# Low parts of expert weights and one-hots on VectorE, reordering copies on ScalarE, in an attention, mixture-of-experts and GLU kernel

## The chip, the cores and the metric

One Trainium2 chip, one core. The metric is the device time of one execution in microseconds (us). TensorE is PE, VectorE is DVE, ScalarE is ACT, GpSimd is POOL, SyncE is SP.

## What is computed

The reference is a chain of three layers on 2304 tokens of width 512 (4 batches of 576):

```python
scores = scale * np.matmul(q, k.transpose(0, 1, 3, 2))
scores = np.where(masks[None], scores, -1e9)      # 4 heads: window 32; 4 heads: dilated by 4
attn = softmax(scores); x = np.matmul(attn, v)    # then heads side by side: (2304, 512)
noisy_logits = x @ w_gate + np.log1p(np.exp(x @ w_noise)) * noise
top2 = np.argpartition(-noisy_logits, 2, axis=1)[:, :2]     # 2 of 8 experts per token, softmax weights
out[mask] += top2_w[mask, k, None] * (np.maximum(x[mask] @ w1[e], 0.0) @ w2[e])
return silu(x @ w_gate2) * (x @ w_val) @ w_out    # GLU, inner width 1536
```

## The kernel before

**Attention** is cut into 36 units (4 batches of 9); a unit has four heads and 128 queries (two blocks of 64, each against 96 keys). `att_step(i)` (L712 on) interleaves three of them, and every engine runs its instructions in the order written: PE scores S(i+1) (L194, L201); DVE row maximum `nm` (L209) and `nb` (L213); PE AV(i-1) (L238); DVE `den`, `rec`, `xs` of unit i-1 (L267 to L273); PE transposes XT(i-2) of `xs` (L284); ACT copies them to `xTb` (L292); PE transposes T(i) of `p` (L227), ACT `pT` (L229); ACT exponentials `p` of unit i+1 (L220). 

**Routing** of each batch (gate logits, two best experts, slots) is a generator, `routing(gi)`; calls of `go(n)` and `pump` between the attention's DVE instructions let it issue n more of its own, so its small DVE operations stand among those of the units. Its last steps build one-hots: per pair (column i of the group, choice k) an `ob` (L463) and an `oa` (L466), which PE multiplies (`s_inv`, L478) to invert the slots. A group has n = 4 or 5 columns, so 2n pairs; POOL builds the last two pairs of each group and DVE the others. `s_rows` (L423 to L455) follows.

**Mixture of experts** runs over steps of one segment (a run of up to 640 slots of an expert) and one eighth f of the inner width. A step's weights `raw` (128x1024) come by DMA (3 buffers) and are split into a high part `whi` (ACT, L173) and a low part `wlo = raw - whi` (L175), 4 buffers each. `moe_step(i)` issues `load_raw(i+5)`, `moe_h(i)` (PE, L657), `hhi` (ACT, L669) and `hlo` (DVE, L670), the token chunks of the next segment (`trans_x`), `split(i+2)` and `moe_y(i-1)` (PE, L696). The low part is DVE's, but POOL's for the four splits that are issued within attention, and for i = 3, 5, 7, 9.

**`trans_x`** reorders a gathered chunk `xg` to `xk` (POOL, L643), transposes it on PE (L608) and makes `xth` (ACT, L616) and `xtl` (DVE, L618). It does so for seven chunks: two of segment 0 (in units 32 and 33, `FIRST_X`), two of segment 1 and three of segment 2. Later segments are turned by DVE and have no such copy.

**Where the work is put** in attention: `LOADS` lists the units in which the first five `raw` are loaded, `SPLITS` those in which the first four are split; the split stands behind the unit's `att_step`, so `whi` is behind the exponentials of the next unit on ACT, and `wlo` ahead of the next unit's `nm` on its engine. The GLU follows after the 88 steps of the experts and is not touched.

Of the kernel before, what the change touches and what calls it, by code (L numbers as in the profile page):

```python
# [8 lines left out]
F32 = mybir.dt.float32  # L9
# [4 lines left out]
AF = mybir.ActivationFunctionType  # L14
OP = mybir.AluOpType
# [25 lines left out]
def attn_moe_glu_kernel(ctx, tc, qT, kT, vB, cst, wgn, noise, wm, wz, out):  # L41
    nc = tc.nc
    V, A, T, G, SP = nc.vector, nc.scalar, nc.tensor, nc.gpsimd, nc.sync
# [96 lines left out]
    iotb = gp.tile([128, 128], BF16, name="iotb")  # L140
    iotc = gp.tile([128, NA * E], BF16, name="iotc")
# [19 lines left out]
    raw, whi, wlo = {}, {}, {}  # L161

    def load_raw(i):
        if i < len(steps):
            s, f = steps[i]
            raw[i] = ring.tile([128, 1024], F32, tag="raw", bufs=3, name="raw")
            SP.dma_start(raw[i], wm[segs[s][0], f])

    def split(i, eng=V):
        if i < len(steps):  # L170
            whi[i] = ring.tile([128, 1024], F32R, tag="whi", bufs=4, name="whi")
            wlo[i] = ring.tile([128, 1024], F32R, tag="wlo", bufs=4, name="wlo")
            A.activation(whi[i], raw[i], AF.Copy)  # L173
            yield
            eng.tensor_tensor(wlo[i], raw[i], whi[i].bitcast(F32), op=OP.subtract)  # L175


    units = []
# [130 lines left out]
    def routing(gi):  # L309
        g0, g1 = groups[gi]  # L310
        n = g1 - g0
        X = {}

        def tl(nm, shape, dt=F32):
            X[nm] = gp.tile(shape, dt, tag="g_" + nm, bufs=1, name="g_" + nm)
            return X[nm]
# [138 lines left out]
            V.tensor_tensor(wm_[:, 0, g0:g1], wm_[:, 0, g0:g1], ov, op=OP.add)  # L455
            yield

        def onehots(eng, pairs):
            if "ob" not in X:
                tl("ob", [128, 2 * n, 128], F16)  # L460
                tl("oa", [128, 2 * n, NA * E], F16)
            for i, k in pairs:
                eng.tensor_scalar(X["ob"][:, 2 * i + k, :], iotb, X["sb"][:, k, i:i + 1], None,  # L463
                                  op0=OP.is_equal)
                yield
                eng.tensor_scalar(X["oa"][:, 2 * i + k, :], iotc, X["ca"][:, k, i:i + 1],  # L466
                                  tokid[:, g0 + i:g0 + i + 1], op0=OP.is_equal, op1=OP.mult)
                yield

        pool = [(i, 1) for i in range(n - 2, n)]  # L470
        mine = [(i, k) for i in range(n) for k in range(2) if (i, k) not in pool]
        order = mine + pool

        def s_inv(pairs):
            iv = X["f"][:, 256:256 + NA * E]
            for pr in pairs:
                j = 2 * pr[0] + pr[1]
                T.matmul(iv, lhsT=X["ob"][:, j, :], rhs=X["oa"][:, j, :], start=pr == order[0],  # L478
                         stop=pr == order[-1], skip_group_check=True)
# [34 lines left out]
        yield NEXT  # L514
        s_rank()
        yield from s_slot()
        for _ in onehots(G, pool):
            pass
        h = len(mine) // 2
        yield from onehots(V, mine[:h])  # L520
        yield NEXT
        A.activation(X["ex"], X["ex"], AF.Exp)
        for _ in range(LAG):
            yield
        s_inv(mine[:h])
        yield from onehots(V, mine[h:])
        yield NEXT
        for _ in range(LAG):
            yield
        s_inv(mine[h:] + pool)  # L530
        yield from s_acc()
        if gi == 3:
            yield NEXT
# [35 lines left out]
    def pump_on(n=99):  # L569
        if route:  # L570
            route[0][1] = True
            pump(n)
# [14 lines left out]
    def by_dve(s):  # L587
        return DVE_SEGS[0] <= s < DVE_SEGS[1]
# [4 lines left out]
    def by_chunk(g):  # L593
        return g.rearrange("p (g k q) -> p k g q", g=4, k=4)

    def spread(g):
        return g.rearrange("p k (g q) -> p k g q", g=4)

    def turned(g, quarter, o=None):

        if quarter:
            flat = g.rearrange("p t c -> p (t c)")
            V.transpose(flat, flat)  # L603
            return g.rearrange("p t (k q) -> p k t q", k=4)
        if o is None:
            o = bank("e").rearrange("p (k q) -> p k q", k=4)
        for c in range(4):
            T.transpose(o[:, c, :] if len(o.shape) == 3 else o[:, c // 2, c % 2, :], g[:, c, :], ident)  # L608
        return o
# [24 lines left out]
    def trans_x(s, a, o=None):  # L634
        e, lo, hi = segs[s]
        if s not in xth:
            xth[s] = mp.tile([128, 4, CAP], F32R, tag="xth", bufs=2, name="xth")
            xtl[s] = mp.tile([128, 4, CAP], F32R, tag="xtl", bufs=2, name="xtl")
        c0 = slice(a * 128 - lo, a * 128 - lo + 128)
        g = xgt.pop((s, a))  # L640
        if not by_dve(s):
            rows, g = g, mp.tile([128, 4, 128], F32, tag="y", bufs=5, name="xk")
            G.tensor_copy(spread(g), by_chunk(rows))  # L643
        src = turned(g, by_dve(s), o)
        yield
        yield from parts(src, xth[s][:, :, c0], xtl[s][:, :, c0], by_dve(s))
# [216 lines left out]
    def moe_step(i):  # L863
        s, f = steps[i]
        last = s == len(segs) - 1
        load_raw(i + 5)
        if i == CVS[0]:
            cv = pools["cv"] = st_cv.enter_context(tc.tile_pool(name="cv", bufs=1, reuse_waits="tile"))
            least.append(cv.tile([128, 1], F32, name="least"))
            V.memset(least[0], 1.125 * 2.0 ** 25)  # L870
        if last and f == 0:
            pools["x2"] = st_x2.enter_context(tc.tile_pool(name="x2", bufs=1, side="right", reuse_waits="tile"))
            load_w2(0, pools["x2"])
            load_w2(1, pools["x2"])
        fg = f - 3 if s == 1 else f
        ft = f - 5 if s == 1 else f - 2
        if not last:
            b0, b1 = segs[s + 1][1] // 128, segs[s + 1][2] // 128
            if 0 <= fg < b1 - b0:
                gather_x(s + 1, b0 + fg)  # L880
        if last and 1 <= f < 4:
            gather_y(f - 1)
        if last and 5 <= f:
            join_y(f - 5)
        if i > 0:
            moe_h(i)
        if i > 2:
            pump_on(3)
        moe_relu(i)
        go(5)  # L890
        tx = trans_x(s + 1, b0 + ft) if not last and 0 <= ft < b1 - b0 else iter(())
        sp = split(i + 2, G if i < 11 and i % 2 else V) if i >= 2 else iter(())
        if by_dve(s + 1):
            next(sp, None)
            next(tx, None)
            next(tx, None)
        else:
            list(tx)
            if last and 6 <= f:
                trans_y(f - 6)  # L900
            next(sp, None)
        if segs[s][2] - segs[s][1] <= LOW:
            list(sp)
            list(tx)
        if i > 0:
            moe_y(i - 1)
            if f == 0:
                moe_out(s - 1)
        if i == 3:
            pump_on(1)  # L910
        go(5)
        if i == 31:
            assert not route
            st_gate.close()
        if i in CVS:
            list(cv_tick(CVS.index(i)))
            if i == CVS[-1]:
                st_cv.close()
        list(tx)
        list(sp)  # L920
# [1 line left out]

    SETS = {(1, 0): (0, 1), (1, 1): (3, 2), (2, 0): (8, 2), (2, 1): (13, 2), (3, 0): (18, 2), (3, 1): (24, 2)}
    coming = {}
    LOADS = (15, 17, 19, 23, 25)
    SPLITS = (20, 22, 24, 26)
    for i in range(-1, NU + 2):
        u = i + 1
        b, r = divmod(u, 9)
        for bt, (i0, di) in SETS.items():  # L930
            if i == i0:
                coming[bt] = load_qkv(*bt)
            if bt in coming and (i - i0) % di == 0:
                next(coming[bt], None)
        if i == 2:
            SP.dma_start(ccon[:, 128:C_MASK], cst[:, 128:C_MASK])
            SP.dma_start(wg, wgn)
            SP.dma_start(nz, noise)
        if 11 <= i < 38:
            if (i - 11) % 9 == 0:  # L940
                route.append([routing((i - 11) // 9), False])
            turn = 99 if len(route) > 1 else 1
        else:
            turn = 0
        if i == NU - 1:
            moe_h(0)
        att_step(i, turn)
        if i >= NU - 1:
            moe_step(i - NU + 1)
        if i < 1:  # L950
            busy(WARM[i + 2])
        if i == 6:
            late_consts()
        if i in LOADS:
            load_raw(LOADS.index(i))
        if i in SPLITS:
            list(split(SPLITS.index(i), G))
        if i == 30:
            gather_x(0, 0)
            gather_x(0, 1)  # L960
# [16 lines left out]
    with tc.If(rv > CAP // 128):  # L977
        with tc.tile_pool(name="ov", bufs=1) as ov:
# [5 lines left out]
            with tc.For_i(0, E, 1) as e:  # L984
                with tc.For_i(CAP // 128, rv, 1) as a:
                    ic = ov.tile([128, 1], I32, tag="ic", name="ic")
                    V.tensor_copy(ic, idx[:, bass.ds(a * E + e, 1)])
                    g = ov.tile([128, DM], F32, tag="xg", name="xg")
# [24 lines left out]
            with tc.For_i(LOW // 128, NT, 1) as t:  # L1013
                for k in range(2):
# [4 lines left out]
                    g = ov.tile([128, DM], F32, tag="xg", name="xg")  # L1019
# [169 lines left out]
```

## Time and profile before

| | |
|---|---|
| three runs | 1068.84, 1066.98, 1057.93 us (median 1066.98) |
| the profiled execution | 1065.96 us |
| its span (first to last instruction) | 1063.9 us, mean granted clock of TensorE 0.984 |
| PE busy | 1024.8 us (96%) |
| DVE busy | 600.0 us (56%) |
| ACT busy | 427.2 us (40%) |
| POOL busy | 331.5 us (31%) |

Times in rows are us from the start of the span. A clock of 1.00 is TensorE's full 2.4 GHz, 0.5 is its lower level, 1.2 GHz. In a row of the timeline the brackets hold the engine's idle time just before the instruction and what ended it; instructions of one kind that follow each other are joined (x4).

### The profile page before, as it was taken

What the parts mean: (1) busy time and instruction counts of PE and PEld (TensorE: products, weight loads), DVE (VectorE), ACT (ScalarE), POOL (GpSimd) and SP (SyncE); (2) the same over time, 40 slices, a digit from 0 to 9 for tenths busy, and PEclk for the clock granted to TensorE, in tenths of its full rate; (3) what the DMA queues carried; (4) which work ended last, traced back from release to release, by engine and by line L of the source; (5) the groups of instructions that cost most, each with busy time, mean ns of one, the idle gap of its engine ahead of it and who ended that gap; (6) DMA issues with size and microseconds to landing.
All of it is one profiled execution on the core that took longest, in us unless ns stands there. A gap on an engine that the chain in (4) does not pass through costs nothing. (4 is left out here: it accounts for less than half of the span.)

```text
span 1063.9 us, 16850 instructions
## 1 busy us (share of the span) xinstructions
PE 1024.8 (96%) x6561; PEld 920.1 (86%) x6562; DVE 600.0 (56%) x1259; ACT 427.2 (40%) x840; POOL 331.5 (31%) x324
## 2 busy tenths in 40 slices
PE   8988988899999999999999999799999999999998
PEld 5776777788999989899989899699999999999997
DVE  3587685468898788897865443134244233343222
ACT  4786543355565555565544322123122122122111
POOL 0023347626343526260001477315126035000000
PEclk8998999999999999999999999899999999999999
DMA  9994355566677777867686586101101101000000
GB/s 252 260 281 148 105 162 179 198 201 187 243 266 254 240 238 242 285 221 238 219 294 223 209 299 228 58 10 40 40 13 43 35 20 40 30 1 1 30 1 30
DMA packets 60980, 161.33 MB, mean 152 GB/s; under 512 B 10048, under 2 KB 17344, under 8 KB 60224
## 3 DMA queue, kind: packets, MB, share of 16 engines
q1 hardware_dynamic: 47904, 120.95, 35.4%
q0 software_dynamic: 12560, 38.82, 11.1%
q8 instruction: 52, 0.85, 0.3%
q10 hardware_dynamic: 432, 0.44, 0.1%
q14 instruction: 32, 0.26, 0.1%
HBM read 121.37 MB, written 38.80 MB: 151 GB/s over the span
## 5 line engine op out<-in xcount | busy, mean ns | idle before, releaser
L591 POOL DMA_INDIRECT xg<-zd,idx x139 | 158.0, 1137 | 168.4 <-DVE xtl L618 127.3
L591 POOL DMA_INDIRECT yg<-zd,row x126 | 122.8, 974 | 200.4 <-DVE yg L844 128.3
L657 PE MATMUL bA<-xth,whi 128*128 128x320 f32 (+2 forms) x452 | 115.9, 314 | 11.9 <-DVE hlo L670 6.1
L657 PE MATMUL bA<-xtl,whi 128*128 128x320 f32 (+2 forms) x452 | 114.9, 312 | 0.2 <-issue 0.2
L657 PE MATMUL bA<-xth,wlo 128*128 128x320 f32 (+2 forms) x452 | 114.6, 311 | 0.0
L1054 DVE TENSOR_TENSOR t<-bB,ex 128x384 f32<-128x384 f32 x36 | 20.1, 558 | 152.6 <-ACT ex L1052 137.8
L669 ACT ACTIVATE hhi<-bA 128x640 fp32r<-128x640 f32 (+2 forms) x73 | 42.4, 581 | 155.7 <-PE bA L657 129.2
L175 DVE TENSOR_TENSOR wlo<-raw,whi 128x1024 fp32r<-128x1024 f32 x80 | 97.2, 1215 | 8.9 <-ACT whi L173 7.7
L657 PEld LDWEIGHTS bA<-xth,whi 128*128 128x128 f32 x452 | 80.6, 190 | 20.8 <-DVE hlo L670 9.2
L173 ACT ACTIVATE whi<-raw 128x1024 fp32r<-128x1024 f32 x88 | 92.7, 1054 | 0.0
L670 DVE SCALAR_TENSOR_TENSOR hlo<-bA,hhi 128x640 fp32r<-128x640 f32 (+2 forms) x73 | 48.9, 669 | 74.8 <-ACT hhi L669 59.1
L657 PEld LDWEIGHTS bA<-xtl,whi 128*128 128x128 f32 x452 | 79.3, 190 | 1.4 <-issue 0.5
L657 PEld LDWEIGHTS bA<-xth,wlo 128*128 128x128 f32 x452 | 79.5, 190 | 0.0
L1052 ACT ACTIVATE ex<-bB 128x384 f32<-128x384 f32 x36 | 17.7, 492 | 151.7 <-PE bB L1046 120.5
L1058 ACT ACTIVATE th<-t 128x384 fp32r<-128x384 f32 x72 | 37.9, 526 | 87.7 <-DVE t L1055 71.8
L1054 DVE TENSOR_TENSOR t<-bA,ex 128x384 f32<-128x384 f32 x36 | 20.1, 558 | 93.3 <-ACT ex L1052 82.3
L1059 DVE TENSOR_TENSOR tl<-t,th 128x384 fp32r<-128x384 f32 x72 | 40.3, 559 | 42.7 <-ACT th L1058 40.9
L1046 PE MATMUL bA<-x2h,wl 128*128 128x384 f32 x288 | 57.7, 340 | 4.6 <-issue 4.6
L1046 PE MATMUL bB<-x2h,wh 128*128 128x384 f32 x288 | 57.3, 341 | 0.0
L1046 PE MATMUL bA<-x2h,wh 128*128 128x384 f32 x288 | 56.5, 338 | 0.3 <-PEq L977 0.3
L1046 PE MATMUL bB<-x2h,wl 128*128 128x384 f32 x288 | 56.4, 337 | 0.0
L1046 PE MATMUL bB<-x2l,wh 128*128 128x384 f32 x288 | 56.3, 337 | 0.0
(233 smaller groups left out, 2353.3 us busy)
## 6 DMA issues: line engine op xcount, KB each, us to landing
raw<-in_wm SPq DMA_DIRECT2D x88, 512.0 KB
r<-in_wz SPq DMA_DIRECT2D x36, 512.0 KB
zd<-y SPq DMA_DIRECT2D x40, 256.0 KB
whd<-cvh SPq DMA_DIRECT2D x36, 256.0 KB
wld<-cvl SPq DMA_DIRECT2D x36, 256.0 KB
wh<-whd POOLq DMA_DIRECT2D x12, 768.0 KB
wl<-wld POOLq DMA_DIRECT2D x12, 768.0 KB
v<-in_vB SPq DMA_DIRECT2D x7, 877.5 KB
```

The costliest lines, as they stand in the source:

```text
L173: A.activation(whi[i], raw[i], AF.Copy)
L175: eng.tensor_tensor(wlo[i], raw[i], whi[i].bitcast(F32), op=OP.subtract)
L591: G.indirect_dma_start(out=g, out_offset=None, in_=src, in_offset=bass.IndirectOffsetOnAxis(ap=ix, axis=0))
L657: T.matmul(hp[:, q, 0:cw], lhsT=wt[:, ws], rhs=xt[:, c, q * cw:q * cw + cw], start=c == 0 and j == 0, stop=c == 3 and j == 2)
L669: A.activation(a3, hp, AF.Relu)
L670: V.scalar_tensor_tensor(l3, hp, 0.0, a3.bitcast(F32), op0=OP.max, op1=OP.subtract)
L1046: T.matmul(p[:, q, 0:LOW], lhsT=w[:, ws], rhs=x[:, c, :], start=c == 0 and j == 0, stop=c == 3 and j == 2, skip_group_check=True)
L1052: A.activation(ex, p[:, 0, 0:LOW], AF.Sigmoid)
L1054: V.tensor_tensor(t, p[:, 0, 0:LOW], ex, op=OP.mult)
L1058: A.activation(a, t, AF.Copy)
L1059: V.tensor_tensor(l, t, a.bitcast(F32), op=OP.subtract)
```

## The change

Every low part is DVE's, every one-hot is DVE's (the pairs are now cut in two equal halves of n), the reordering copy `xk` is ACT's, and the loads and splits within attention lie in other units.

```diff
-    def split(i, eng=V):
+    def split(i):
...
             A.activation(whi[i], raw[i], AF.Copy)
             yield
-            eng.tensor_tensor(wlo[i], raw[i], whi[i].bitcast(F32), op=OP.subtract)
+            V.tensor_tensor(wlo[i], raw[i], whi[i].bitcast(F32), op=OP.subtract)
...
-                eng.tensor_scalar(X["ob"][:, 2 * i + k, :], iotb, X["sb"][:, k, i:i + 1], None,
+                V.tensor_scalar(X["ob"][:, 2 * i + k, :], iotb, X["sb"][:, k, i:i + 1], None,
...
-        pool = [(i, 1) for i in range(n - 2, n)]
-        mine = [(i, k) for i in range(n) for k in range(2) if (i, k) not in pool]
-        order = mine + pool
+        order = [(i, k) for i in range(n) for k in range(2)]
...
-        for _ in onehots(G, pool):
-            pass
-        h = len(mine) // 2
-        yield from onehots(V, mine[:h])
+        yield from onehots(order[:n])
...
-        s_inv(mine[:h])
-        yield from onehots(V, mine[h:])
+        s_inv(order[:n])
+        yield from onehots(order[n:])
...
-        s_inv(mine[h:] + pool)
+        s_inv(order[n:])
...
-            G.tensor_copy(spread(g), by_chunk(rows))
+            A.activation(spread(g), by_chunk(rows), AF.Copy)
...
-        sp = split(i + 2, G if i < 11 and i % 2 else V) if i >= 2 else iter(())
+        sp = split(i + 2) if i >= 2 else iter(())
...
-    LOADS = (15, 17, 19, 23, 25)
-    SPLITS = (20, 22, 24, 26)
+    LOADS = (13, 15, 17, 20, 23)
+    SPLITS = (18, 19, 27, 28)
...
-            list(split(SPLITS.index(i), G))
+            list(split(SPLITS.index(i)))
```

On DVE, around the end of unit 18, the kernel before has the end of group 0's one-hots, the maximum of unit 20 (`nm`), `den` of unit 18 and the copy of the inverted slots:

```order
L463 TENSOR_SCALAR g_ob<-iotb,g_sb 128x128
L466 TENSOR_SCALAR g_oa<-iotc,g_ca,ccon 128x144
L209 TENSOR_REDUCE nm<-bA 128x4
L213 TENSOR_SCALAR nb<-nm 128x4
L267 TENSOR_SCALAR den<-bd 128x4
L484 COPY inva<-bf 128x144
```

The changed kernel has there (its line numbers are 2 to 5 lower in these functions):

```order
L463 TENSOR_SCALAR g_ob<-iotb,g_sb 128x128
L175 TENSOR_TENSOR wlo<-raw,whi 128x1024
L209 TENSOR_REDUCE nm<-bA 128x4
L466 TENSOR_SCALAR g_oa<-iotc,g_ca,ccon 128x144
L213 TENSOR_SCALAR nb<-nm 128x4
L267 TENSOR_SCALAR den<-bd 128x4
L482 COPY inva<-bf 128x144
```

The first `wlo` has come to stand ahead of `nm` and of the group's last `oa`. One unit later the second `wlo` stands in the same way ahead of the next `nm`.

On ACT, in units 31 to 33, the kernel before has the exponentials `p`, the copies `xTb`, the first chunk's `xth` and `pT`:

```order
L220 ACTIVATE p<-bA,nb 128x96 x4
L292 ACTIVATE xTb<-bd 128x2x128
L616 ACTIVATE xth<-bB 128x4x128
L229 ACTIVATE pT<-bc 96x512
L220 ACTIVATE p<-bB,nb 128x96 x4
L292 ACTIVATE xTb<-be 128x2x64 x2
```

The changed kernel has there:

```order
L220 ACTIVATE p<-bA,nb 128x96 x4
L638 ACTIVATE xk<-xg 128x512
L292 ACTIVATE xTb<-bd 128x2x128
L611 ACTIVATE xth<-bB 128x4x128
L229 ACTIVATE pT<-bc 96x512
L220 ACTIVATE p<-bB,nb 128x96 x4
L638 ACTIVATE xk<-xg 128x512
```

Each `xk` has come in behind the exponentials of the unit in which its chunk is transposed; before, it is not on ACT but on POOL, behind the gathers.

## Rows read from the trace of the kernel before

**Rows 1.** Windows: stretch, length; busy PE, PEld, DVE, ACT, POOL; clock, DMA share, GB/s.
```profile
53.00:68.00 15.00, 14.62 (x273) 11.31 (x272) 14.04 (x78) 12.56 (x43) 3.00 (x4) 1.00 0.93 284
...
74.00:93.00 19.00, 12.13 (x216) 9.34 (x215) 18.30 (x63) 12.27 (x37) 10.01 (x7) 0.98 0.60 179
93.00:100.00 7.00, 7.00 (x79) 4.94 (x80) 4.97 (x28) 3.69 (x12) 2.74 (x3) 0.58 0.72 214
...
136.00:157.00 21.00, 16.58 (x115) 14.27 (x114) 18.68 (x51) 9.18 (x15) 11.12 (x7) 1.00 0.50 153
```
**Rows 2.** Timeline of POOL: start, length, engine, line, operation, output<-inputs [idle before <-releaser].
```profile
74.58 2.36 POOL L175 TENSOR_TENSOR wlo<-raw,whi 128x1024 fp32r<-128x1024 f32 x1 [3.64 <-ACT whi L173]
```
**Rows 3.** Timeline of DVE, around units 18 and 19 and under that instruction of POOL.
```profile
61.40 0.24 DVE L463 TENSOR_SCALAR g_ob<-iotb,g_sb 128x128 f16<-128x128 bf16 x1
...
61.79 0.24 DVE L463 TENSOR_SCALAR g_ob<-iotb,g_sb 128x128 f16<-128x128 bf16 x1
...
64.36 0.55 DVE L209 TENSOR_REDUCE nm<-bB 128x4 f32<-128x384 f32 x1
...
67.06 0.42 DVE L273 TENSOR_TENSOR xs<-be,rec 128x256 f32<-128x256 f32 x1
...
74.61 2.39 DVE L363 SCALAR_TENSOR_TENSOR g_cc<-g_qq,ccon 128x40 f32<-128x40 f32 x1
...
78.54 0.20 DVE L363 SCALAR_TENSOR_TENSOR g_cc<-g_qq,ccon 128x40 f32<-128x40 f32 x1
```
**Rows 4.** Timeline of PE, at the places of the change.
```profile
62.50 0.38 PE L284 MATMUL be<-ident,xs 128*128 128x128 f32 x2
...
67.84 0.44 PE L284 MATMUL be<-ident,xs 128*128 128x128 f32 x2
...
79.50 0.18 PE L383 MATMUL bf<-g_mb,trib 128*128 128x40 bf16 x1 [2.04 <-DVE g_mb L376]
...
90.77 0.22 PE L478 MATMUL bf<-g_oa,g_ob 128*128 128x144 f16 x1 [1.17 <-DVE g_oa L466]
...
105.56 0.66 PE L608 MATMUL bB<-ident,xk 128*128 128x128 f32 x4
...
108.23 0.66 PE L608 MATMUL bA<-ident,xk 128*128 128x128 f32 x4
...
123.88 0.66 PE L608 MATMUL be<-ident,xk 128*128 128x128 f32 x4
127.89 0.66 PE L608 MATMUL be<-ident,xk 128*128 128x128 f32 x4
142.12 0.39 PE L657 MATMUL bA<-xth,whi 128*128 128x256 f32 x1 [1.73 <-DVE hlo L670]
```
**Rows 5.** Groups of instructions by line: busy us, mean ns of one | idle before.
```profile
L175 DVE TENSOR_TENSOR wlo<-raw,whi 128x1024 fp32r<-128x1024 f32 x80 | 97.2, 1215 | 8.9 <-ACT whi L173 7.7 <-issue 0.9
L173 ACT ACTIVATE whi<-raw 128x1024 fp32r<-128x1024 f32 x88 | 92.7, 1054 | 0.0
L175 POOL TENSOR_TENSOR wlo<-raw,whi 128x1024 fp32r<-128x1024 f32 x8 | 19.0, 2374 | 30.3 <-ACT whi L173 30.3
...
L837 ACT ACTIVATE xk<-yg,w 128x512 f32<-128x512 f32 x3 | 2.2, 726 | 4.5 <-DMA yg<-zd,row 4.5
```
**Rows 6.** Timeline of ACT, the exponentials and a relu at the places of the change.
```profile
61.35 1.01 ACT L220 ACTIVATE p<-bB,nb 128x96 f32<-128x96 f32 x4
...
63.88 1.00 ACT L220 ACTIVATE p<-bA,nb 128x96 f32<-128x96 f32 x4
...
105.51 1.01 ACT L220 ACTIVATE p<-bA,nb 128x96 f32<-128x96 f32 x4
...
109.59 1.04 ACT L220 ACTIVATE p<-bB,nb 128x96 f32<-128x96 f32 x4 [1.00 <-DVE xtl L618]
...
128.34 0.38 ACT L669 ACTIVATE hhi<-bA 128x256 fp32r<-128x256 f32 x1
```

More of the change, by code (lines that the diff above doesn't have):

```diff
@@ L456, in s_rows, with onehots @@
             yield
-        def onehots(eng, pairs):
+        def onehots(pairs):
             if "ob" not in X:
@@ L462, in onehots @@
             for i, k in pairs:
-                eng.tensor_scalar(X["ob"][:, 2 * i + k, :], iotb, X["sb"][:, k, i:i + 1], None,
+                V.tensor_scalar(X["ob"][:, 2 * i + k, :], iotb, X["sb"][:, k, i:i + 1], None,
                                   op0=OP.is_equal)
                 yield
-                eng.tensor_scalar(X["oa"][:, 2 * i + k, :], iotc, X["ca"][:, k, i:i + 1],
+                V.tensor_scalar(X["oa"][:, 2 * i + k, :], iotc, X["ca"][:, k, i:i + 1],
                                   tokid[:, g0 + i:g0 + i + 1], op0=OP.is_equal, op1=OP.mult)
                 yield
-        pool = [(i, 1) for i in range(n - 2, n)]
-        mine = [(i, k) for i in range(n) for k in range(2) if (i, k) not in pool]
-        order = mine + pool
+        order = [(i, k) for i in range(n) for k in range(2)]
         def s_inv(pairs):
```

## The prediction, made before the changed kernel ran

> **What bounds the kernel now.** I read the busy times first: PE is busy for 96% of the span, so a change pays or costs only where PE waits. Cut into windows, the trace shows where that is [rows 1]. In 53 to 68 us PE is busy 14.62 of 15.00 us, but DVE is nearly full as well (14.04), and ACT has little room (12.56). In 74 to 93 PE is busy only 12.13 of 19.00, so it idles 6.87, with DVE at 18.30 of 19. In 136 to 157 it idles 4.42 (21.00 less 16.58), with DVE at 18.68 of 21. The instructions that the change touches are all issued before the experts' fourth segment, so it is decided in the first fifth of the span, and there DVE is the engine that PE waits for.
>
> Then the timelines of POOL and DVE side by side, for why DVE is so full. At 74.58 POOL starts a low part of 2.36 us [rows 2]; at 74.61 DVE starts a tiny operation that takes 2.39 us, and the same operation takes 0.20 at 78.54 [rows 3]. DVE is held for as long as POOL's low part runs, about 2.2 us each. PE pays some time later: 2.04 us of idle at 79.50, 1.17 at 90.77, 1.73 at 142.12 [rows 4].
>
> The Trainium skill has this as a rule ("SBUF — State Buffer", section "Who interferes with whom"): DVE and GpSimd share one pair of ports as an exclusive lock, held for a whole instruction, while PE and ACT wait for no one. The rows just given agree with it (2.39 against 0.20). By that rule alone every low part taken from POOL is a gain; that is the first rival below, worked out from rows.
>
> **The change part by part.** PE's instructions are the same in number. Removed: eight low parts of 2374 ns on POOL, which come to DVE at 1215 ns each [rows 5]; eight one-hot pairs come to DVE, at 0.39 us each from one `ob` to the next in a run of them (61.40 to 61.79) [rows 3]; seven copies `xk` go from POOL to ACT, where the same shape costs 726 ns (L837) [rows 5]. The high parts stay ACT's, 1054 ns each [rows 5]. Against the stalls of 2.2 us DVE's total falls; the question is what stands behind each new instruction.
>
> 1. *Splits 0 and 1, in units 18 and 19.* In the fullest stretch. Exp of unit 19 ends at 61.35 + 1.01 = 62.36 [rows 6]; then the high part, to 63.41; then the low part on DVE, to 64.63. Behind it in DVE's order stand `nm` (0.55 [rows 3]) and the last `oa` of group 0, so to about 65.4. PE's last one-hot product waits for that `oa`, and XT, which started at 62.50 [rows 4], waits behind it: 2.9 us. In the next unit it repeats. The exp that stood at 63.88, 1.38 behind XT, comes to 66.8 and ends 1.00 later [rows 6]; high part to 68.85, low part to 70.1; behind it DVE has everything from `nm` (64.36) to the end of `xs` (67.06 + 0.42), 3.12 us [rows 3], so `xs` is there at 73.2 and XT at 73.3 in place of 67.84 [rows 4]: 5.5 in all. Lower bound: only DVE's added work counts, 2 x 1.215 + 2 x 0.39 = 3.2, less its idle of 0.96 in that window: 2.2. Upper bound: the pairs come on top, 6.3. I take **+5.5**, since the orders of DVE and PE leave no way round.
>
> The Trainium skill speaks against just this step ("Perfetto Trace Analysis", section "Optimizing Scalar/DVE Operations"): where DVE is saturated, work may better be handed from it, to ScalarE or even GpSimd, though the shared port can spoil the latter. The 14.04 of 15.00 us [rows 1] says that DVE is saturated in the stretch in which it is given two splits; the sum by the rule has the sign of the +5.5.
>
> 2. *Three stalls in 74 to 93.* The wait of 2.04 at 79.50 goes whole; it follows the first stall. Of the other idle there, 6.87 - 2.04 - 1.17 = 3.66 (the 1.17 belongs to part 3), some waits follow the second stall and some are PE waiting for one-hots that DVE makes one by one, which it still does. I take 1.7, somewhat under half: **-3.7**; bounds -2.0 and -5.7.
>
> 3. *Splits 2 and 3, in units 27 and 28.* The one at 27 takes the place of the third stall: 1.215 plus a pair and the wait for the high part, against 2.2 that go; +0.2. The one at 28 stands ahead of `nm` and of the routing's small operations that `xs` follows; that is a low part and a short wait for its high part, 1.4. DVE has room after it (4.97 of 7.00 in 93 to 100 [rows 1]). Sum **+1.6**; bounds -1.2 (the 1.17 goes and both fit in gaps) and +3.
>
> 4. *Copies in units 32 and 33.* PE did not wait for POOL's copies (no bracket at 105.56 and 108.23 [rows 4]); on ACT each is behind an exp. First: exp ends at 105.51 + 1.01 = 106.52 [rows 6], the copy at 107.25, and PE wanted it at 105.56 [rows 4]: +1.7, of which I take 1.6 for the overlap of the four exps. Second: exp ends at 109.59 + 1.04 = 110.63 [rows 6], the copy 0.73 later at 111.36, PE wanted it at 108.23 [rows 4]: 3.1. Some comes back, since that exp also held up PE's next transposes: 2.8. Sum **+4.4**; bounds 0 (hidden) and +4.8.
>
> 5. *Copies in the experts' part.* They stand behind `hhi`. The first of segment 1 is wanted at 123.88 [rows 4] just as a `hhi` ends: +0.7, the copy. The second is wanted at 127.89 [rows 4], the `hhi` ends at 128.34 + 0.38 = 128.72 [rows 6], the copy at 129.45: +1.5. Three of segment 2 with shorter queues, 0.4 each. **+3.4**; bounds 0 and +4.4.
>
> 6. *The experts' steps 5 to 9.* Three stalls of 2.2 leave DVE (6.6), three low parts (3.6) and two pairs (0.8) come: 2.2 less work where PE idles 4.42, of which 1.73 is one wait for `hlo` right behind a stall. The low part now stands behind that step's `hlo`, not across it. **-2.5**; bounds 0 and -4.4.
>
> 7. *The clock.* After the idle stretches of 74 to 93 the granted clock falls: 93 to 100 has a mean of 0.58, so mostly the lower level, 1.2 GHz. PE is busy 7.00 of 7.00 us there [rows 1]; at full clock the same work would take 7.00 x 0.58 = 4.1, so one such fall costs up to 2.9. The waits of parts 1 and 4 are new idle, two of them longer than the 2.04 that was not followed by a fall (the window 74 to 93 has 0.98). I take one new fall, with part of the old one gone: **+2.0**; bounds -2.9 (none is left) and +11.6 (four new ones).
>
> Sum: 5.5 - 3.7 + 1.6 + 4.4 + 3.4 - 2.5 + 2.0 = +10.7. On the profiled execution, 1065.96, that is 1076.7. Its time stands 0.1% under the median of the three runs, so it can be set beside that.
>
> **The rivals.**
>
> *A: the stalls were the whole trouble (other side).* DVE without stalls is ahead of PE, takes low parts in its gaps, and the copies find ACT idle. Then all idle of 74 to 93 and 136 to 157 goes, and the fall after it: 6.87 + 4.42 + 2.9 = 14.2, so 1051.8. For it: the stalls are as long as POOL's instruction, and DVE's total falls. Against: the 14.04 of 15.00 in the stretch that gets two splits, where no stall is to be had back. It decides if XT of unit 17 is less than 1 us late.
>
> *B: each new wait is followed by the lower clock.* Four falls at 2.9 in place of part 7's 2.0: 11.6 - 2.0 = 9.6 on top, 1086.3. For it: the idle before 93. Against: the 2.04 at 79.50 had no such sequel.
>
> *C: the copies cost nothing*, because PE comes to them late after the earlier delays while ACT does not. Without parts 4 and 5 (7.8): 1068.9, no change. Against: both are measured from exp and `hhi`, which wait for PE themselves and so are late with it.
>
> **How the numbers follow.** About 1%, or 10.7 us, is what a measurement of this kernel can tell from no change: bounds 1056.3 and 1077.7 about the median. My forecast, 1076.7, gets 0.40, with its own range of 1071 to 1083, half of it above 1077.7; A 0.21, C 0.21, B 0.18. Faster: A but for its nearest cases, 0.18. Same: 0.03 of A, C, and half of the forecast, 0.44. Slower: the other half and B, 0.38. The range leaves out some of A's better half and the worst of B: 1055 to 1088.
>
> **What would show it.** Right: PE waits of 2 to 3 us for one-hots and `xs` near 62 and 68 us; XT of unit 19 some 5 us later; no DVE instruction of 2.3 us; waits of PE for `xk` of ACT in units 32 and 33 and after two `hhi`; PE idle in 136 to 157 (shifted) below 2.5. Wrong: `wlo` of unit 18 done before PE wants the last one-hot, or ACT making `xk` ahead of the exp that stands before it; a clock of 0.5 in more stretches than the forecast's one would speak for B.

## The result and the profile after

Over 22 runs each, the kernel before has a median of 1063.55 us (1050.8 to 1073.0), the changed one 1069.9 us (1062.91 to 1075.53). The ratio is 1.0115, with a 95% interval of 1.0088 to 1.0143: slower by about 12 us. The medians of all runs lie only 6.35 us apart: the ratio leaves slow runs out, and only the kernel before has any (nine of its 22 are more than 1.5% above its fastest). The forecast was 1076.7 us against 1065.96, +10.7 us or +1.0%. Between 6 and 12 us the size is therefore taken from the stages below.

The windows of the changed kernel, for the stretches of [rows 1] and two more (columns as there):

```profile
53.00:68.00 15.00, 12.08 (x164) 8.90 (x168) 11.17 (x52) 9.62 (x30) 0.00 (x0) 0.77 0.82 244
60.88:65.65 4.77, 4.77 (x49) 3.10 (x49) 2.18 (x11) 3.37 (x9) 0.00 (x0) 0.50 0.69 210
...
74.00:93.00 19.00, 14.45 (x264) 11.39 (x260) 15.57 (x77) 14.61 (x48) 0.00 (x0) 1.00 0.80 228
93.00:100.00 7.00, 5.01 (x52) 3.35 (x56) 5.47 (x26) 1.13 (x3) 3.67 (x4) 0.60 0.29 83
...
113.00:120.00 7.00, 6.66 (x83) 5.67 (x84) 4.95 (x25) 4.05 (x13) 0.00 (x0) 0.76 0.05 19
...
136.00:157.00 21.00, 19.84 (x141) 16.67 (x140) 15.71 (x49) 10.16 (x19) 0.00 (x0) 1.00 0.41 128
```

The idle of 74 to 93 and 136 to 157 has shrunk (19.00 - 14.45 = 4.55 and 1.16, from 6.87 and 4.42), but 53 to 68 has gone from 14.62 busy at a clock of 1.00 to 12.08 at 0.77, with 60.88 to 65.65 wholly at the lower level (0.50), and 93 to 100 has a low clock as before. Where PE waited, from its timeline:

```profile
60.81 0.28 PE L476 MATMUL bf<-g_oa,g_ob 128*128 128x144 f16 x1 [2.79 <-DVE g_oa L466]
...
78.68 0.18 PE L383 MATMUL bf<-g_mb,trib 128*128 128x40 bf16 x1 [0.30 <-DVE g_mb L376]
...
94.99 1.19 PE L321 MATMUL bf<-xTb,wg 128*32 128x288 f32 x8 [3.77 <-DVE inva L485]
...
107.71 0.66 PE L603 MATMUL bB<-ident,xk 128*128 128x128 f32 x4 [1.46 <-ACT xk L638]
113.34 0.66 PE L603 MATMUL bA<-ident,xk 128*128 128x128 f32 x4 [2.90 <-ACT xk L638]
...
129.66 0.66 PE L603 MATMUL be<-ident,xk 128*128 128x128 f32 x4 [0.73 <-ACT xk L638]
...
135.08 0.66 PE L603 MATMUL be<-ident,xk 128*128 128x128 f32 x4 [1.32 <-ACT xk L638]
148.18 0.39 PE L652 MATMUL bA<-xth,whi 128*128 128x256 f32 x1 [0.60 <-DVE hlo L665]
```

The waits of [rows 4] behind stalls (2.04, 1.73) have shrunk to 0.30 and 0.60; six new ones are there, five of them above a microsecond. What DVE did at the new places, and the operation that a stall had held for 2.39 us [rows 3]:

```profile
58.84 1.23 DVE L175 TENSOR_TENSOR wlo<-raw,whi 128x1024 fp32r<-128x1024 f32 x1 [0.93 <-ACT whi L173]
59.98 0.55 DVE L209 TENSOR_REDUCE nm<-bA 128x4 f32<-128x384 f32 x1
60.45 0.31 DVE L466 TENSOR_SCALAR g_oa<-iotc,g_ca,ccon 128x144 f16<-128x144 bf16 x1
...
64.89 1.22 DVE L175 TENSOR_TENSOR wlo<-raw,whi 128x1024 fp32r<-128x1024 f32 x1 [2.29 <-ACT whi L173]
...
68.72 0.42 DVE L273 TENSOR_TENSOR xs<-be,rec 128x256 f32<-128x256 f32 x1
...
75.98 0.20 DVE L363 SCALAR_TENSOR_TENSOR g_cc<-g_qq,ccon 128x40 f32<-128x40 f32 x1
...
88.56 1.23 DVE L175 TENSOR_TENSOR wlo<-raw,whi 128x1024 fp32r<-128x1024 f32 x1 [1.60 <-ACT whi L173]
92.83 1.23 DVE L175 TENSOR_TENSOR wlo<-raw,whi 128x1024 fp32r<-128x1024 f32 x1 [1.14 <-ACT whi L173]
94.63 0.30 DVE L485 TENSOR_TENSOR inva<-bf,inva 128x144 f32<-128x144 f32 x1
```

In front of each of the four low parts DVE is idle for its high part on ACT, 5.96 us in all, with work queued behind. The group of all copies shows that they are cheap in themselves:

```profile
L638 ACT ACTIVATE xk<-xg 128x512 f32<-128x512 f32 x7 | 4.4, 628 | 0.0
```

**A ruler for what follows.** Spans of whole runs differ for reasons that have nothing to do with the change (two profiles of the kernel before have spans of 1063.9 and 1038.8). So I measure from one fixed instruction to another: XT(n) is the start of PE's transposes of unit n (L284), h(i) that of `hhi` in step i. The marks of the second profile of the kernel before (run e8):

```profile
57.45 0.38 PE L284 MATMUL bd<-ident,xs 128*128 128x128 f32 x2
...
68.61 0.44 PE L284 MATMUL bd<-ident,xs 128*128 128x128 f32 x2
...
84.84 0.38 PE L284 MATMUL be<-ident,xs 128*128 128x128 f32 x2
98.33 0.44 PE L284 MATMUL bd<-ident,xs 128*128 128x128 f32 x2
...
118.42 0.38 PE L284 MATMUL be<-ident,xs 128*128 128x128 f32 x2
131.09 0.37 ACT L669 ACTIVATE hhi<-bA 128x256 fp32r<-128x256 f32 x1
162.47 0.38 ACT L669 ACTIVATE hhi<-bB 128x256 fp32r<-128x256 f32 x1 [1.49 <-PE bB L657]
174.70 0.49 ACT L669 ACTIVATE hhi<-bA 128x384 fp32r<-128x384 f32 x1 [2.05 <-PE bA L657]
```

These are XT(16), (20), (25), (28), (35), h(4), (13) and (16); differences of neighbours give a line of this table (us), in which every run stands in the same way:

```
                                   splits 0,1  routing  splits 2,3  copies,   copies,   experts'  copies,
                                               1        (new place) attention segment 1 low parts segment 2
                                   XT16-20     20-25    25-28       28-35     XT35-h4   h4-13     h13-16
before, first profile              11.17       16.25    13.64       20.09     12.51     31.34     17.44
before, run e8                     11.16       16.23    13.49       20.09     12.67     31.38     12.23
changed, first profile             17.01       12.71    16.44       25.22     13.92     28.14     21.18
changed, run e11                   17.00       12.70    16.34       25.25     13.93     28.14     23.99
e1  changed, copies on POOL        17.01       12.70    16.31       20.33     11.61     28.12     12.24
e2  changed, old places            11.95       19.09    10.18       26.36     13.95     28.12     14.17
e3  e1 and e2                      11.95       18.75    11.44       20.34     11.62     28.12     12.23
e4  before, copies on ACT          11.16       16.23    13.62       27.93     13.94     31.93     14.16
e5  changed, split 1 in unit 20    15.66       12.71    15.84       25.37     13.94     28.11     14.18
e6  changed, low part a unit late  12.40       12.70     9.69       25.23     13.96     28.11     14.17
e7  e3 and a unit late             11.85       14.98     9.75       20.33     11.61     28.12     12.23
e9  e1 and a unit late             12.40       12.71    10.54       20.59     11.61     28.13     12.25
e10 changed, copies on ACT earlier 17.01       12.71    16.36       20.33     11.62     28.13     12.25
e12 before, experts' low on DVE    11.17       16.23    12.37       20.09     12.64     28.19     29.72
```

For the same code most entries repeat within 0.2 us. XT(25) to (28) doesn't: e12 has 12.37 there against 13.64 and 13.49 of the kernel before, e3 11.44 against e2's 10.18, e9 10.54 against e6's 9.69, each pair with the same code up to XT(28). A difference of about a microsecond in that column says nothing. The last one also holds waits that came in some executions and not in others (17.44 and 12.23 for the same kernel). With 14.17 there, as in e2, the changed kernel's stages sum to 127.6 us against 117.25: +10.4.

### The profile page after: what moved, and what is told of

It reads as the page before. It is cut to its first block, busy times and chain, and to the rows that moved or that the text cites. A ratio compares the mean times of both kernels' runs of the same rounds, so it can differ in the third digit from the quotient of the medians.

```text
span 1068.2 us, 16836 instructions
## 1 busy us (share of the span) xinstructions
PE 1024.0 (96%) x6562; PEld 921.0 (86%) x6562; DVE 597.5 (56%) x1283; ACT 430.5 (40%) x847; POOL 293.8 (28%) x293
## 5 line engine op out<-in xcount | busy, mean ns | idle before, releaser
L175 DVE TENSOR_TENSOR wlo<-raw,whi 128x1024 fp32r<-128x1024 f32 x88 | 107.0, 1216 | 15.5 <-ACT whi L173 14.6
L1047 ACT ACTIVATE ex<-bA 128x384 f32<-128x384 f32 x36 | 17.6, 490 | 105.9 <-PE bA L1041 95.0
L1041 PEld LDWEIGHTS bB<-x2h,wh 128*128 128x128 f32 x288 | 52.4, 191 | 4.7 <-issue 1.7
```

What stands on the lines that cost most here:

```text
L175: V.tensor_tensor(wlo[i], raw[i], whi[i].bitcast(F32), op=OP.subtract)
L1041: T.matmul(p[:, q, 0:LOW], lhsT=w[:, ws], rhs=x[:, c, :], start=c == 0 and j == 0, stop=c == 3 and j == 2, skip_group_check=True)
L1047: A.activation(ex, p[:, 0, 0:LOW], AF.Sigmoid)
```

## The experiments

All ratios are to the kernel before on the same chip, with 95% intervals. The theory: the new waits are a matter of where an instruction stands in an engine's order (the low part behind a high part, the copy behind exponentials), and stretches at the lower clock follow the longest. The rivals: DVE is simply full, the copies are hidden, or the stalls were all that mattered.

**e1: copies back on POOL.**

```diff
-            A.activation(spread(g), by_chunk(rows), AF.Copy)
+            G.tensor_copy(spread(g), by_chunk(rows))
```

> The changed kernel with the seven reordering copies xk back on POOL. Theory (the copies on ACT cost what PE waits for them): the waits of 1.46, 2.90, 0.73, 1.32 and 0.17 us, 6.6 in all, go; against the kernel before +5.6 us, ratio about 1.005. Rival (the copies cost nothing, PE would be held there anyway): ratio stays at 1.0115.

Measured: ratio 1.0012 (0.9995 to 1.0029). This is below the 1.005 that was expected: the copies cost more than the 6.6 us of their waits. The table has 4.9 less in attention, 2.3 in segment 1 and, against the 14.17 of e2 with the same copies, 1.9 in segment 2.

**e2: the old places.**

```diff
-    LOADS = (13, 15, 17, 20, 23)
-    SPLITS = (18, 19, 27, 28)
+    LOADS = (15, 17, 19, 23, 25)
+    SPLITS = (20, 22, 24, 26)
```

> The changed kernel with loads and splits within attention in the units of before (15, 17, 19, 23, 25 and 20, 22, 24, 26), all on DVE. Theory (the places 18, 19, 27, 28 are the fullest for DVE and ACT): the one-hot wait of 2.79 us goes, the lower clock behind it too, and part of the 3.77 us wait in unit 27; 4 to 8 us of the 12 go, ratio 1.004 to 1.008. Rival (DVE is full wherever it gets them): ratio 1.010 or more.

Measured: 1.0075 (1.0053 to 1.0097). 5.1 and 6.2 us go at the new places, 6.4 of them come back in XT 20 to 25, where the splits now stand. A good part of the price moves with the splits. Another 1.1 us comes in XT 28 to 35, with the same copies as in the changed kernel: here the clock fell already behind the first wait for `xk`.

```profile
105.44 0.66 PE L603 MATMUL bB<-ident,xk 128*128 128x128 f32 x4 [1.46 <-ACT xk L638]
```

```profile
107.40:109.10 1.70, 1.70 (x21) 1.11 (x19) 1.56 (x8) 1.25 (x3) 0.00 (x0) 0.50 0.03 8
```

**e3: both edits.**

> Both of the two edits before: copies on POOL and the places of before, low parts and one-hots on DVE. Theory: the two gains add, 10 to 14 of the 12 us go, ratio 0.998 to 1.002. Rival (the stalls were the whole trouble and only these two edits hid it): 5 us or more below the kernel before, ratio 0.995 or less.

Measured: 0.9972 (0.9959 to 0.9984), a little better than the kernel before. The gains add. The rival's 0.995 is not reached. The one-hots on DVE, which no run moves alone, are in this run too, and so are not by themselves what made the changed kernel slower.

**e4: the kernel before with only the copies on ACT.**

> The kernel before with only the copies xk on ACT. Theory: PE waits for each as in the changed kernel, +6.6 us, ratio 1.006, with waits of 1.4 and 2.9 us in units 32 and 33 and 0.7 and 1.3 in segment 1. Rival (they cost only beside the other edits): ratio 1.000 to 1.002.

Measured: 1.0093 (1.0068 to 1.0118), more than forecast. PE's timeline, and three windows of the run:

```profile
104.75 0.66 PE L608 MATMUL bB<-ident,xk 128*128 128x128 f32 x4 [1.46 <-ACT xk L643]
110.39 1.12 PE L608 MATMUL bA<-ident,xk 128*128 128x128 f32 x4 [2.91 <-ACT xk L643]
```

```profile
100.00:115.00 15.00, 10.64 (x148) 8.54 (x140) 7.30 (x32) 8.36 (x27) 0.00 (x0) 0.84 0.12 36
110.40:115.00 4.60, 4.60 (x44) 3.66 (x44) 2.75 (x13) 1.52 (x5) 0.00 (x0) 0.50 0.08 28
115.00:136.00 21.00, 18.29 (x167) 15.80 (x160) 12.05 (x57) 10.35 (x28) 4.85 (x6) 0.87 0.36 119
```

The waits are those of the changed kernel within a hundredth (1.46 and 2.91), so they need none of the other edits. The stage is 7.8 us longer, though, not 4.4: the clock is low behind the second wait (0.50 in 110.40 to 115), and the transposes that end it last 1.12 us in place of 0.66.

**e5: the second split a unit later.** `SPLITS = (18, 20, 27, 28)`.

> The changed kernel with the second split one unit later, in unit 20 in place of 19. In the changed kernel XT of unit 16 to XT of unit 20 took 17.0 us against 11.2 before; one wait of 2.79 is seen, the rest has no wait but a lower clock. Theory C (clock): the rest is the lower clock that follows the wait, so it stays: about 17 us again, clock near 0.8 in the 20 us behind unit 16. Theory D (the second low part holds DVE, as the prediction had it): about 14 us, some of it moved to the next unit. The time hardly differs from the changed kernel's under either (ratio to the kernel before 1.007 to 1.013).

Measured: 1.0075 (1.0050 to 1.0100); XT(16) to (20) 15.66, between the two theories. Over the 11.16 of the kernel before stand 4.5: the wait of 2.79, and 1.7 without any wait, nearly all of it in XT(17) to (18), at a low clock:

```profile
60.76:64.95 4.19, 4.19 (x49) 2.64 (x48) 2.81 (x18) 2.54 (x8) 0.00 (x0) 0.59 0.55 157
```

With the second low part in unit 19, the changed kernel takes 1.35 more: 0.58 in this stretch, XT(17) to (18), where it has 0.50 in place of 0.59 and no wait either, and the rest in XT(18) to (19). How much of that is the low part and how much a longer stay at the lower clock, this run does not separate. Both theories had a part.

**e6: the low part one unit behind its high part.**

```diff
+        for lo in late:
+            list(lo)
+        late = []
         if i in SPLITS:
-            list(split(SPLITS.index(i)))
+            late = [split(SPLITS.index(i))]
+            next(late[0])
```

> The changed kernel with each of the four low parts in attention one unit behind its high part, so that DVE doesn't wait for ACT with the low part ahead of the next maximum. Theory (the price of units 18 and 19 is DVE standing behind ACT, and the lower clock behind that wait): the wait of 2.79 us falls under 1.5, the clock stays at 1.00 in units 17 to 20, the wait of 3.77 in unit 27 shortens; 4 to 7 us below the changed kernel, ratio to the kernel before 1.005 to 1.009. Rival (DVE is simply full there): the waits only move by a unit, less than 2 us gained.

Measured: 0.9994 (0.9975 to 1.0013). More than the theory had: 4.6 us in splits 0 and 1 and 6.8 in splits 2 and 3, with the same work on the same engines. Two waits, the first low part and three windows:

```profile
60.10 0.22 PE L476 MATMUL bf<-g_oa,g_ob 128*128 128x144 f16 x1 [0.63 <-DVE g_oa L466]
...
87.76 0.69 PE L321 MATMUL bf<-xTb,wg 128*32 128x288 f32 x8 [1.63 <-DVE inva L485]
```

```profile
61.74 1.22 DVE L175 TENSOR_TENSOR wlo<-raw,whi 128x1024 fp32r<-128x1024 f32 x1
```

```profile
55.00:75.00 20.00, 18.72 (x335) 14.57 (x332) 17.95 (x84) 16.98 (x55) 0.00 (x0) 1.00 0.89 265
83.00:92.00 9.00, 7.32 (x136) 5.20 (x136) 8.42 (x40) 7.78 (x23) 2.99 (x3) 1.00 0.68 172
90.00:100.00 10.00, 8.54 (x145) 6.71 (x144) 6.76 (x28) 6.99 (x23) 3.02 (x3) 1.00 0.50 145
```

2.79 has become 0.63, 3.77 has become 1.63, and the clock is 1.00 in all three windows, even in 83 to 92, where units 26 and 27 now lie, in which the kernel before had its fall. None of the four low parts waits for ACT any more. "DVE is simply full" is refuted: it had stood waiting for ACT. The loads lie here as in the changed kernel, so their new units are not the cause either.

**e7: e3 with the low parts a unit late.**

> As the run with copies on POOL and the old places (ratio 0.997), with each low part in attention one unit behind its high part. Theory: waits for one-hots, xs and the like in 73 to 92 us (7 us in that run) shrink by 2 to 4 us; ratio 0.993 to 0.996. Rival (DVE's own one-hots and small operations are what PE waits for): 0.996 to 0.999.

Measured: 0.9919 (0.9893 to 0.9946): 1032.2 us against 1041.91, faster than both kernels and somewhat more than was expected.

**e8: the kernel before, for its profile.**

> The kernel before, unchanged, for a profile from this chip: how far the stretches that the change doesn't touch differ between two profiles. Expected: XT of unit 16 to XT of unit 35 takes 61.1 us as in the first profile, within 1 us; what is left of the difference between the two chips lies elsewhere.

Measured: XT(16) to (35) 60.97 us (118.42 - 57.45), against 61.15 in the first profile. The spans differ by 25.1 us all the same; 5.2 of these lie in h(13) to h(16), which has no idle stretch in this execution. One thing differs that the prediction leaned on. The wait of 2.04 is here again, and the clock fell behind it. In the first profile, in the same stretch of the work 2.5 us later (second window), it had not:

```profile
76.97 0.18 PE L383 MATMUL bf<-g_mb,trib 128*128 128x40 bf16 x1 [2.04 <-DVE g_mb L376]
```

```profile
79.00:81.00 2.00, 1.91 (x33) 1.50 (x34) 2.00 (x4) 1.35 (x6) 1.49 (x1) 0.50 0.04 13
```

```profile
81.50:83.50 2.00, 1.21 (x33) 0.88 (x33) 2.00 (x4) 1.38 (x6) 1.54 (x1) 1.00 0.02 9
```

**e9: e1 with the low parts a unit late.**

> The changed kernel with copies on POOL and each low part in attention one unit behind its high part, in the new places (18, 19, 27, 28). Theory (the stages add: 12.4, 12.7, 9.7, 20.3, 11.6, 28.1 and 12.2 us from XT of unit 16 to hhi of step 16, as each was in a run that had this piece, 107.1 in all against 117.3 of the kernel before): -10 us, ratio 0.990. Rival (the places themselves are bad, and the old ones win): ratio above the 0.992 of the run with the old places, by 0.002 or more.

Measured: 0.9926 (0.9887 to 0.9965); the stages sum to 108.2 us (107.1 expected), against 108.9 for e7. The interval holds the theory's 0.990 and the rival's 0.994. So old and new places cannot be told apart once DVE does not stand behind ACT.

**e10: copies on ACT, one unit or step earlier.** The copy is cut out of `trans_x`, and called ahead of the unit's or step's own work:

```diff
+        if i + 1 in FIRST_X:
+            copy_x(0, FIRST_X.index(i + 1))
         att_step(i, turn)
...
         list(sp)
+        if not last and 0 <= ft + 1 < b1 - b0 and not by_dve(s + 1):
+            copy_x(s + 1, b0 + ft + 1)
```

> The changed kernel with each copy xk still on ACT, but issued one unit or step earlier, ahead of the exponentials or the hhi that it stood behind. Theory (the price of the copies is their place in ACT's order, with the lower clock behind the waits): PE's waits for xk go, 8 to 10 us below the changed kernel, ratio to the kernel before 1.000 to 1.003. Rival (ACT has no room for 0.73 us more in these units and steps): under 4 us gained, ratio 1.006 or more, other waits in place of those for xk.

Measured: 1.0004 (0.9959 to 1.0049). ACT's copy of the second chunk and PE's transposes:

```profile
109.95 0.64 ACT L631 ACTIVATE xk<-xg 128x512 f32<-128x512 f32 x1
```

```profile
109.11 0.66 PE L603 MATMUL bB<-ident,xk 128*128 128x128 f32 x4
111.77 0.66 PE L603 MATMUL bA<-ident,xk 128*128 128x128 f32 x4
```

The copy is done at 110.59, over a microsecond before PE wants it, and no wait for `xk` is left. The three stages of copies are those of e1, with POOL, within 0.01 us. ACT had the room; only the place was wrong.

**e11: the changed kernel again.**

> The changed kernel as it is, for its ratio and its profile on this chip. By the sum of stages (17.0, 12.7, 16.4, 25.3, 13.9, 28.1 and 14.2, 127.6 against 117.3 us): +10.4 us, ratio 1.010. A ratio under 1.007 would mean that the waits near 175 to 205 us of the first chip make up a part of the difference there.

Measured: 1.0128 (1.0070 to 1.0186). Six of seven stages repeat within 0.1. The seventh, 23.99, holds waits such as the kernel before has in its first profile (17.44); how much of its excess is the change's is left open.

**e12: only the experts' low parts on DVE.** In the kernel before, `split(i + 2)` in place of `split(i + 2, G if i < 11 and i % 2 else V)`.

> The kernel before with only the low parts of the experts' steps 3, 5, 7 and 9 on DVE, one-hots, splits in attention and copies as before. Theory (three stalls of DVE go where PE waited 1.73 and 1.87 us for hlo): hhi of step 4 to hhi of step 13 takes about 28.5 us in place of 31.4, -2.5 to -3 us, ratio 0.997 to 0.998. Rival (the low parts on DVE cost as much as the stalls did): ratio 1.000.

Measured: 1.0005 (0.9955 to 1.0055), too wide to decide by the time. The stage decides: h(4) to h(13) takes 28.19 us in place of 31.4, all that the full change gains there. Of the whole time nothing can be said: h(13) to h(16) was 29.72 in this profile.

## Why the prediction was right, point by point

The time, the sign and nearly the size were right: +10.7 forecast, +10.4 by stages, +12 by the ratio. The range, 1055 to 1088, also holds no change at all, so the time alone says little for the mechanism; the stages say more. The terms were not all of the right size.

1. *Splits 0 and 1, +5.5:* the stage grew by 5.84. The first wait was forecast at 2.9 and measured 2.79, by the path that was given (exp, high part, low part, `nm`, the last `oa`). **The second half of this term was paid in another way**: a further wait of 2.6 us behind the second low part was forecast, and PE waited at most 0.30 for `xs` there (in e1, where the stage is the same). DVE was as late as the walk had it: `xs` ends at 69.14, 13.65 us behind XT(16), against 13.2 by the walk. But PE came late itself, and so did not wait. XT(17) to (18) took 4.77 us in place of 2.65 with no wait in it, at a clock of 0.50. The walk moved PE at full clock. XT(16) to (19) of the changed kernel, and XT(16) and (18) of the kernel before:

```profile
55.49 0.38 PE L284 MATMUL bd<-ident,xs 128*128 128x128 f32 x2
60.88 0.63 PE L284 MATMUL be<-ident,xs 128*128 128x128 f32 x2
65.65 0.69 PE L284 MATMUL bd<-ident,xs 128*128 128x128 f32 x2
69.20 0.44 PE L284 MATMUL be<-ident,xs 128*128 128x128 f32 x2
```

```profile
59.97 0.38 PE L284 MATMUL bd<-ident,xs 128*128 128x128 f32 x2
65.15 0.44 PE L284 MATMUL bd<-ident,xs 128*128 128x128 f32 x2
```

   The rule of the Trainium skill on saturation ("Perfetto Trace Analysis", section "Optimizing Scalar/DVE Operations"), set beside this term, had the sign; but e6, with the same load on DVE and 12.40 in place of 17.01, shows that most of the cost was not DVE's load.
2. *Stalls in 74 to 93, -3.7:* measured -3.5 (16.25 to 12.71).
3. *Splits 2 and 3, +1.6:* measured +2.8. **The place was missed**: the wait is not for `xs` but for `inva`, 3.77 us. `inva` (94.63) stands behind the fourth low part (92.83), and PE's next gate product shares its bank. With e6 the stage is 4 us under that of the kernel before, so what it had grown by went with the place of the low parts: DVE behind ACT, and the fall after.
4. *Copies in attention, +4.4:* the two waits are 1.46 + 2.90 = 4.36. The stage grew by 5.1, in e4 by 7.8; the clock is low behind the second wait in both (0.76 in 113 to 120, and e4's 0.50).
5. *Copies among the experts, +3.4:* 0.73 and 1.32 measured for 0.7 and 1.5 in segment 1. Against the kernel before, as in the other points, the two stages grew by 1.4 (12.51 to 13.92) and 1.9 (12.23 to e2's 14.17), 3.3 in all. Against e1, which differs in the copies alone, they cost 2.3 + 1.9 = 4.2: something else in the change gave 0.9 back in segment 1, and what it was is open. Segment 2, forecast as 1.2, was too low.
6. *Experts' low parts, -2.5:* measured -3.2, from e12 by the low parts alone.
7. *Clock, +2.0:* **mis-sized at its place.** One new fall was forecast, with part of the old one gone. Stretches at a low clock came behind the three longest new waits: 2.79 (0.50, 2.1 us in XT(17) to (18) alone), 3.77 (0.60 in 93 to 100, about where the old one was) and 2.90 (0.76). The first of them is the second half of point 1, so that points 1 and 7 count one delay twice there. Without the clock, points 1 to 6 were forecast at 8.7, and their stages grew by 10.4; the 2.0 happens to cover the 1.7 that is missing, of which 1.2 is point 3 and 0.7 point 4, while point 6 was 0.7 better.

*Rival A* (the stalls were all) was wrong in the changed kernel: 2.79 is above the 1 us that was set as its point of decision. The idea in it was sound for e6 and e7, in which DVE does take the low parts in gaps. *Rival B* (a fall behind each wait, +20.3 in all) is refuted by its number, but not in its idea: low stretches came behind three of the new waits where the forecast had one, and what was set against it, the 2.04 without a sequel, does not hold in e8. Behind 1.46 there was no fall in the changed kernel, and the price behind 2.90 was 0.7 us in one run and 3.5 in another, not 2.9 each. *Rival C* (copies hidden) is refuted by e1 and e4.

The forecast held because its main step, walking the four new low parts and seven copies through the orders of ACT and DVE up to the PE instruction that wants them, gave every term its sign, and the first one-hot wait (2.9 against 2.79) and the four waits for `xk` up to segment 1 within 0.2 us. It missed the place of the wait in point 3 and took for a wait of PE what was a lower clock in point 1. That the sum lies within 0.3 us of the stages is in part luck: the terms were off by -0.7 to +1.2 us, and a clock put down as a term of its own made up for it.

## What to carry to other kernels

An instruction that goes to another engine has two prices: its duration, and the wait of everything queued behind it while it waits for its own input. Here the second was the larger. Issuing the low parts one unit later took 11.4 us off the stages (4.6 + 6.8), and issuing the copies one unit or step earlier took off 9.1 (with e2's 14.17 for the last stage of the changed kernel), with the same work on the same engines. So when work is moved between engines, issue it where its input is already there (here one unit behind its producer), or ahead of the long work that it would stand behind, and walk each new wait to the instruction that sets the end.

## What was not expected of the hardware

- The lower clock does not follow every wait alike. Behind 2.9 us in the same place it cost 0.7 us in one run (28 to 35: 25.2, of which 4.4 are waits) and 3.5 in another (27.93). Behind the same 1.46 in unit 32 the clock stayed at 1.00 in both profiles of the changed kernel and in e5 and e6, and fell in e2 (0.50 in 107.4 to 109.1); behind the same 2.04 it stayed at 1.00 in the first profile of the kernel before and fell in the second (0.50 in 79 to 81). So the length of a wait alone did not tell what the clock did.
- The copy of 128x512 took ACT 628 ns, where POOL had taken 785 on average [a group of the kernel before's profile, `L643 POOL COPY xk`] and the row taken for its price 726 [rows 5].
- Two profiles of the same kernel on two chips differ by 25 us of span. One of the differences is 17.44 against 12.23 us in h(13) to h(16), which came with idle stretches of PE; on one and the same chip (e9 to e12) that stage took from 12.25 to 29.72. The cause was not looked for.
